# A fused attention and gated feed-forward kernel on one core: a new hand-written order for all engines, with the unread matmuls of the first block placed differently

## The chip, the cores and the metric

The kernel runs on one core of one Trainium2 chip. The metric is the device time of one execution in microseconds (us). The engines of the core are named as in the profile: PE (TensorE, the matrix engine), PEld (its weight loads, which overlap its matmuls), DVE (VectorE), ACT (ScalarE), POOL (GpSimd) and SP (SyncE, which here only issues DMAs). Each engine works through its own row of instructions in the order in which it was given them, and the engines wait for one another through semaphores.

## The reference

The computation has two stages, both in float32 at the ends. The weights arrive as float64 words. With B = H = 8, S = 576, D = 64, d_model = 512 and d_ff = 1536:

```python
k_p = k.reshape(B, H, 72, 8, D).mean(axis=3)      # keys pooled by 8: 576 -> 72
v_p = v.reshape(B, H, 72, 8, D).mean(axis=3)
scores = matmul(q, k_p.T) / sqrt(D)               # 576 x 72 per head
attn = exp(scores - max(scores)); attn /= sum(attn) + 1e-9
x = matmul(attn, v_p)                             # put together: 4608 x 512
gate = 1 / (1 + exp(-(x @ w_gate)))               # 512 -> 1536
val = x @ w_val
out = (gate * val) @ w_out                        # 1536 -> 512
```

## The kernel before, in words

**Tiling.** The 4608 tokens are cut into 9 blocks of 512. A block's attention works on four pairs p of heads (128 rows) and on two halves hf of the queries. In the code's names: `keys` (DVE sums 8 neighbours), `put` (ACT writes the pooled keys of a pair into a block-diagonal tile `kbd`), `sc` (PE's scores: 4 matmuls of 144 columns for half a block), `max` (DVE), `exp` (ACT), `sum`, `main`, `rest` (DVE: the sums of the exponentials, their reciprocals and the scaling), `turn` and `rturn` (PE's transposes), `hi`, `lo` (ACT and DVE split a float32 value in two float32r parts), `av` (PE: attention times values), `x` (ACT copies a block's x out of PSUM). A float32 product of the feed-forward stage is three float32r matmuls, high by high, high by low and low by high.

**Block 0 alone.** `first_pass` computes block 0 from attention to output, reads and converts the weights meanwhile (`lw` loads 1 MB of float64 words, `conv` and `kw` make float32r parts of it on ACT and DVE, `mm.i.f` is chunk f of the product with w_gate, i = 0, or w_val, i = 1, in four chunks; `gate.f` its sigmoid, `h.f` the product, `acc.f` the second layer), and does the attention of blocks 1 and 2. Words are written with their indices: `sc.0.1.1` is the scores of block 0, pair 1, half 1, and `first.k.i` is the first pass's load i of kind k (kind 0: the keys k0..k3; 1: the queries q0..q3; 2: a table of ones for sums over tokens; 3: block 0's values, four pieces and a rest).

**Blocks 1 to 8 in four rounds** of two blocks each. In a round the first layer is done by products of the Strassen kind: m = 1..7 for gate (G) and value (V) and for each of six pairs p of chunks, each product 6 matmuls of 512 columns into a `chain` bank. Their operands are `xo` tiles (sums of quarters of the two blocks' x, each combined on DVE, copied by ACT and split by DVE), and the weights come back from DRAM by `reload` in groups A to D into a ring of six `parts` buffers: a load waits until the product that used the buffer last is done. The second layer (`second_sums`) goes over 21 units (m, q) of 12 matmuls into `acc` banks, its weights loaded into three `oparts` buffers and its operands `hs` made by ACT and DVE, i = 0..20, two units ahead. The next round's x operands (`combine`, `parts_of`) and the attention of later blocks stand between.

**The order.** All this code doesn't issue anything by itself. Every engine instruction is recorded as a unit of a `Book`; matmuls that belong together are one unit. Buffers and PSUM banks are handed out in the order of recording, which in `first_pass` is the list of words `ORDER`. At the end the units are issued in another order, that of a table of numbers, `LATER`, one number for each unit:

```python
    with tc.manual_schedule(engines={e.engine for e in engines}):
        for n in LATER.split() or range(len(book.units)):
            for taken in book.units[int(n)]:
                taken.issue()
```

So `LATER` alone sets each engine's row, the DMA issues on SP's and POOL's included, while what a unit computes and where it puts it stay as recorded.

**The unread matmuls.** When a word of `first_pass` gets its PSUM bank, `bank_for` can record matmuls ahead of its own, 128 x 128 in float32 of a zero tile or the identity, into that same bank. Nobody reads what they write: the word's own first matmul starts the bank anew. How many is in `UNREAD`, a count by word; each is a unit of its own and leaves two records of PE in the profile.

```python
            x = kbd[RING - 1][:, :P] if now[0].startswith("sc.0") else ident
            for _ in range(UNREAD.get(now[0], 0)):
                nc.tensor.matmul((t[:, 0] if len(shape) == 3 else t)[:, :P], lhsT=x, rhs=x, start=True, stop=True)
```

Every instruction that goes through the `Book` shows in the profile with line 319, where it is issued; which one it is is told by its tiles.

## Time and profile before

| | before |
|---|---|
| runs: median of 3 (lowest to highest) | 934.22 us (932.6 to 936.99) |
| the profiled execution | 933.27 us |
| its span in the profile | 931.5 us |
| granted TensorE clock, mean | 0.999 |
| instructions | 12557 |
| PE busy | 918.0 us, 99% of the span |
| DVE busy | 695.0 us, 75% |
| ACT busy | 572.4 us, 61% |
| POOL busy | 24.1 us, 3% |

The span runs from the first to the last recorded work of the profiled execution; the 1.8 us between it and the execution's time lie around that. Busy shares are averages over the whole span, and the stages differ: what counts is read by stretches of time and from the waits of each engine. An idle time in brackets stands ahead of the instruction that ended it, with what released it.

### The profile page before, as it was taken

The numbers are of one execution on the slowest core, as the hardware profiler recorded it, in microseconds if no ns is written. First come the engines' busy times: TensorE is split into PE (matmuls) and PEld (weight loads), VectorE is DVE, ScalarE is ACT, GpSimd is POOL, SyncE is SP. The second block draws the span as 40 slices with busy tenths as digits, with TensorE's granted clock in tenths as the row PEclk, the third lists the DMA queues.
The fourth block names the chain that finished last, engine by engine and source line by source line (L and its number), as shares of the span: only waits on it lengthen the run. The fifth ranks groups of instructions, "written<-read, shape, count | busy, mean of one in ns | idle before, by whom it ended". The sixth has DMA issues, their size and how long they took to land.

```text
span 931.5 us, 12557 instructions
## 1 busy us (share of the span) xinstructions
PE 918.0 (99%) x4375; PEld 756.0 (81%) x4375; DVE 695.0 (75%) x1062; ACT 572.4 (61%) x1044; POOL 24.1 (3%) x59
## 2 busy tenths in 40 slices
PE   8999999999999999999999999999999999999998
PEld 7778788887888878888888888888888878888886
DVE  6998888899999997976789956464768573544763
ACT  7999998679989764665575636443554353234442
POOL 1000000011121000000000000000000000000000
PEclk9999999999999999999999999999999999999999
DMA  9999496778889757787667567545456675566266
GB/s 341 372 354 346 164 392 226 254 264 304 289 303 340 265 192 262 265 301 243 210 212 235 191 223 232 191 166 186 156 193 203 216 235 191 177 198 191 94 212 192
DMA packets 90367, 223.13 MB, mean 240 GB/s; under 512 B 9536, under 2 KB 28480, under 8 KB 88768
## 3 DMA queue, kind: packets, MB, share of 16 engines
q1 hardware_dynamic: 85184, 203.97, 64.9%
q0 software_dynamic: 5120, 18.35, 5.1%
q8 instruction: 35, 0.57, 0.2%
q14 instruction: 28, 0.23, 0.1%
HBM read 168.81 MB, written 53.48 MB: 239 GB/s over the span
## 4 chain that ended last, share of the span: by engine, by line
PE 92%; ACT 5%; DMA 2%; DVE 1%; issue 0%; POOL 0%; ACTq 0%; POOLq 0%
PE chain L319 54%; PE acc L319 27%; PE sc L319 4%; PE av L319 4%; PE tp L319 2%; ACT e L319 1%; DMA parts<-keptV0C 1%; DMA oparts<-keptS 1%; ACT w L319 1%; ACT L319 1%; DMA oparts<-keptO 0%; ACT raw L319 0%; ACT y L319 0%; PE vp L319 0%; ACT parts L319 0%
## 5 line engine op out<-in xcount | busy, mean ns | idle before, releaser
L319 PE MATMUL chain<-xo,parts 128*128 128x512 f32 x2316 | 558.6, 394 | 2.9 <-ACT y L319 1.4
L319 PEld LDWEIGHTS chain<-xo,parts 128*128 128x128 f32 x2316 | 427.2, 188 | 93.4 <-ACT y L319 2.1
L319 PE MATMUL acc<-hs,oparts 128*128 128x512 f32 (+1 forms) x1011 | 235.3, 390 | 0.8 <-DMA oparts<-keptO 0.5
L319 PEld LDWEIGHTS acc<-hs,oparts 128*128 128x128 f32 x1011 | 188.2, 188 | 41.6 <-issue 1.4
L319 DVE TENSOR_TENSOR hs<-h,hs 128x1024 fp32r<-128x1024 f32 x52 | 63.3, 1221 | 37.9 <-ACT hs L319 37.5
L319 ACT CAST hs<-h 128x1024 fp32r<-128x1024 f32 x52 | 54.6, 1053 | 52.6 <-PE acc L319 51.4
L319 DVE TENSOR_TENSOR y<-chain,sG 128x512 f32<-128x512 f32 x69 | 47.2, 686 | 45.6 <-PE chain L319 32.3
L319 DVE TENSOR_TENSOR y<-chain,sV 128x512 f32<-128x512 f32 x69 | 47.2, 686 | 37.3 <-PE chain L319 25.8
L319 ACT COPY sV<-chain 128x512 f32<-128x512 f32 x69 | 40.3, 586 | 52.4 <-PE chain L319 48.6
L319 ACT COPY sG<-chain 128x512 f32<-128x512 f32 x69 | 40.4, 586 | 48.3 <-PE chain L319 47.7
L319 ACT ACTIVATE gate<-y 128x512 f32<-128x512 f32 x69 | 43.2, 631 | 39.7 <-DVE y L319 35.2
L319 ACT CAST hs<-s 128x1024 fp32r<-128x1024 f32 x36 | 37.9, 1054 | 39.8 <-PE acc L319 24.2
L319 ACT ACT_TABLE_LOAD x47 | 60.3, 1283 | 1.4 <-DVE y L319 0.5
L319 DVE TENSOR_TENSOR hs<-s,hs 128x1024 fp32r<-128x1024 f32 x36 | 44.0, 1221 | 14.6 <-ACT hs L319 14.4
L319 DVE TENSOR_TENSOR h<-y,gate 128x512 f32<-128x512 f32 x69 | 47.4, 689 | 3.8 <-ACT gate L319 1.8
L319 PE MATMUL sc<-kbd,raw 128*128 128x144 f32 (+1 forms) x260 | 41.0, 295 | 1.0 <-ACT other L319 0.7
L319 PEld LDWEIGHTS sc<-kbd,raw 128*128 128x128 f32 (+1 forms) x260 | 33.5, 177 | 9.8 <-issue 2.8
L319 PE MATMUL acc<-oparts,hs 128*128 128x512 f32 x144 | 37.8, 399 | 0.1
L319 DVE TENSOR_REDUCE m<-sc 128x4 f32<-128x288 f32 x48 | 21.7, 452 | 14.3 <-PE sc L319 14.0
L319 PEld LDWEIGHTS acc<-oparts,hs 128*128 128x128 f32 x144 | 26.3, 188 | 5.5 <-ACT pr L319 0.3
L319 DVE TENSOR_TENSOR h<-h 128x256 f32<-128x256 f32 (+2 forms) x39 | 28.3, 728 | 0.7
L319 ACT ACTIVATE gate<-chain 128x512 f32<-128x512 f32 x23 | 13.8, 599 | 18.9 <-PE chain L319 18.5
(193 smaller groups left out, 1026.0 us busy)
## 6 DMA issues: line engine op xcount, KB each, us to landing
oparts<-keptS SPq DMA_DIRECT2D x48, 512.0 KB, 4.1
oparts<-keptO SPq DMA_DIRECT2D x72, 256.0 KB, 3.5
raw<-in_wgv SPq DMA_DIRECT2D x12, 1024.0 KB, 8.7
out<-o SPq DMA_DIRECT2D x35, 256.0 KB, 4.4
raw<-in_kT SPq DMA_DIRECT2D x28, 288.0 KB, 4.8
raw<-in_qT SPq DMA_DIRECT2D x29, 256.0 KB, 4.4
raw_o<-in_wo SPq DMA_DIRECT2D x12, 512.0 KB, 6.7
keptO<-oparts SPq DMA_DIRECT2D x12, 512.0 KB, 3.8
```

Source lines behind the costliest of these rows:

```text
L319: return self._book.take(lambda: f(*args, **named))
```

## The change

`ORDER`, all functions and all tiles stay as they are. Two tables are new.

`UNREAD` has other counts. In all there are 49 unread matmuls instead of 44, so the book has 3737 units instead of 3732:

```diff
 UNREAD = {
-    "sc.0.1.1": 10, "sc.0.1.0": 1, "sc.0.0.1": 1, "sc.0.2.0": 5, "sc.0.3.1": 7, "sc.0.3.0": 2, "sc.1.0.0": 1,
-    "rturn.0.1": 5, "av.0.3": 1, "mm.0.0": 1, "mm.0.1": 5, "mm.1.0": 2, "mm.1.1": 1, "mm.0.2": 1, "sc.1.1.0": 1,
+    "sc.0.1.1": 1, "sc.0.1.0": 1, "sc.0.0.1": 4, "sc.0.0.0": 2, "sc.0.2.1": 1, "sc.0.2.0": 2, "sc.0.3.1": 3,
+    "rturn.0.0": 2, "turn.0.0": 1, "turn.0.1": 4, "sc.0.3.0": 5, "av.0.0": 1, "rturn.0.1": 2, "turn.0.3": 3,
+    "turn.0.2": 2, "av.0.3": 1, "mm.0.0": 1, "av.0.2": 2, "mm.0.1": 1, "mm.1.0": 2, "mm.1.1": 2, "mm.0.2": 3,
+    "mm.1.2": 1, "sc.1.1.0": 1, "sc.1.1.1": 1,
 }
```

`LATER` is a new table throughout (its numbers can't be compared by eye, since every unit behind a changed count has another number):

```diff
 LATER = """
-2 17 15 11 34 5 10 35 19 14 6 36 12 8 3 37 18 4 7 38 16 9 39 13 28 40 41 20 42 43 24 46 58 90 25 91 92 23 26 93 94 79
...
+3705 3706 3707 3709 3713 3710 3711 3712 3714 3722 3715 3719 3720 3717 3716 3723 3721 3718 3724 3725 3728 3729 3730
+3726 3733 3735 3734 3727 3736 3731 3732
 """
```

Read back into names, the two tables put the engines' rows like this. Unread ones aside, the two rows of an engine hold the same units.

| row | before | after |
|---|---|---|
| PE, from its start | 21 unread, sc.0.1.1, sc.0.1.0, 2 unread, sc.0.0.1, sc.0.0.0, 1 unread, sc.0.2.0, sc.0.2.1, 2 unread, sc.0.3.1, sc.0.3.0 | 14 unread, sc.0.1.1, sc.0.1.0, sc.0.0.1, sc.0.0.0, sc.0.3.1, 4 unread, sc.0.2.1, sc.0.2.0, 8 unread, sc.0.3.0, turn.0.0, turn.0.1 |
| SP, from its start | k1, k0, q1, q3, q0, k2, k3, q2, lv.1.0, lw.0.0, constants, first.3.0 | k1, q1, k3, k0, q0, q2, q3, k2, first.3.4, constants, lv.1.0, first.3.0, lw.0.0 |
| DVE, from its start | keys.0.1, keys.0.0, max.0.1.1, max.0.1.0, keys.0.2 | keys.0.1, keys.0.3, keys.0.0, max.0.1.1, max.0.1.0, max.0.0.1, max.0.0.0, keys.0.2 |
| ACT, from its start (two instructions a put) | put.0.1, put.0.0, exp.0.1.1 | put.0.1, put.0.3, put.0.0, exp.0.1.1 |
| POOL, from its start | a kbd fill, then vl, vh, kbd fills | a vh fill, then the kbd fills among the others |

Of the units that were there before, unread matmuls aside, 776 of PE's 1021, 822 of ACT's 995, 871 of DVE's 1061, 371 of SP's 556 and 28 of POOL's 55 have another place in their row, on the mean 3.7, 3.2, 2.8, 1.6 and 1.8 places away. The mean is taken over a row's units that can be matched by name. Further on, these places differ: in the first pass mm.1.2 goes ahead of mm.1.3; in the second sums of the first round unit m 6, q 1 ahead of m 2, q 0; around the turn from the third to the fourth round the product G, p 0, m 5 goes into the second sums' m 7, five places ahead on PE, the load of V, p 0, group C goes twelve places ahead on SP, and two combinations with the splits of their results go between the operands i = 9 to 13 on DVE; in the last unit of the last round the bank that is copied in one piece comes last instead of the bank that is copied in halves.

## The prediction

> **What bounds the kernel now.** I read the page's engine totals first, then busy time by stage, then what the matrix engine waited for, then the first microseconds row by row.

> ```profile
> span 931.5 us, 12557 instructions
> ...
> PE 918.0 (99%) x4375; PEld 756.0 (81%) x4375; DVE 695.0 (75%) x1062; ACT 572.4 (61%) x1044; POOL 24.1 (3%) x59
> ```
> ```profile
> 10.00:60.00 50.00, 44.99 (x245) 35.52 (x245) 47.70 (x88) 47.45 (x113) 0.00 (x0) 1.00 1.02 380
> 60.00:140.00 80.00, 78.78 (x392) 64.50 (x391) 68.61 (x112) 76.73 (x157) 0.00 (x0) 1.00 0.82 300
> 140.00:310.00 170.00, 169.16 (x819) 138.68 (x818) 158.66 (x277) 142.46 (x286) 21.60 (x40) 1.00 0.80 284
> 310.00:931.50 621.50, 616.07 (x2865) 508.27 (x2863) 416.97 (x582) 302.23 (x482) 0.00 (x0) 1.00 0.63 207
> ```
> ```profile
> PE sc L319 <- ACT early L319: 1.7, 1, 1.7
> ...
> PE chain L319 <- DMA parts<-keptV0C: 0.9, 1, 0.9
> ```

> The second fence gives busy microseconds and instructions of PE, its weight loads, DVE, ACT and POOL in four stretches, then the granted clock, the DMA share and GB/s; the third PE's waits: in total, how often, the longest. PE is idle for only 931.5 - 918.0 = 13.5 us of the whole span, so a new order can win little past the early stage: from 310 us on PE lacks 5.4 us of being always busy. The stage from 10 to 140 us is another matter. ACT is busy for 47.45 of 50 and 76.73 of 80 us there, DVE for 47.70 of 50, and the DMA engines are full to 60 us; PE's busy time there still holds unread matmuls. So early on ACT sets the pace, with DVE close behind; from about 140 us PE does.

> The profiled execution took 933.27 us (span 931.5); the median of the runs is 934.22, that is 0.95 more. I sum against 933.27 and add 0.95 at the end.

> **Part 1: the head start.**

> ```profile
> 0.73 0.22 POOL L319 MEMSET kbd<- 128x144 f32 x1 [0.29 <-POOLq L1454]
> ...
> 0.89 0.20 POOL L319 MEMSET vl<- 128x128 f32 x1
> 1.01 6.94 PE L319 MATMUL sc<-kbd 128*128 128x128 f32 x42 [1.01 <-POOL kbd L319]
> 7.79 1.15 PE L319 MATMUL sc<-kbd,h 128*128 128x144 f32 x8
> 2.12 0.43 SPq L319 DMA_DIRECT2D early<-in_qT  x1
> 3.45 1.53 DVE L319 TENSOR_REDUCE early<-h 128x72 f32<-128x576 f32 x2 [2.58 <-DMA h<-in_kT]
> 8.48 0.95 DVE L319 TENSOR_REDUCE early<-sc 128x4 f32<-128x288 f32 x2 [3.50 <-PE sc L319]
> 4.30 0.53 ACT L319 ACTIVATE kbd<-early 64x72 f32<-64x72 f32 x2 [2.06 <-DVE early L319]
> 8.97 1.45 ACT L319 ACTIVATE e<-sc,early 128x72 f32<-128x72 f32 x6 [3.36 <-DVE early L319]
> ```
> ```profile
> h<-in_kT SPq DMA_DIRECT2D x4, 288.0 KB, 3.8
> h<-in_qT SPq DMA_DIRECT2D x3, 256.0 KB, 4.2
> ```
> ```profile
> 1.00:5.20 4.20, 4.19 (x19) 4.20 (x20) 1.50 (x2) 1.87 (x5) 2.02 (x14) 1.00 0.76 251
> 5.20:7.78 2.58, 2.58 (x25) 2.58 (x24) 0.00 (x0) 0.40 (x2) 0.00 (x0) 1.00 1.05 382
> ```

> The first of these fences goes engine by engine (start, length, and in brackets the idle time ahead); the second gives KB and microseconds from issue to landing. Now 21 unread matmuls (42 records) stand ahead of the first score. Its keys were placed at 4.30 + 0.53 = 4.83 us, and PE has no gap before 7.79: the fillers hold the score back, and DVE (3.50 us) and ACT (3.36 us) wait for it. The new row has 14 fillers, 28 records. PE starts 0.89 - 0.73 = 0.16 us later, since a vh fill now precedes the first kbd fill on POOL. By the two windows a record takes 4.20 / 19 = 0.22 us up to 5.2 us and (7.78 - 5.20) / (42 - 19) = 0.11 us after. So 18 records fill 1.17 to 5.2, and the other 10 take 1.1: the first scores can start at 6.3 instead of 7.8. q1 is now the second load, at about 1.2 us, and lands about 4.2 later, 5.4: in time.

> What DVE does meanwhile: keys.0.3 now precedes keys.0.0, and k0 is the fourth load (the fourth issues at 2.12; plus 3.8 to 4.2 it is there at about 6.2). keys.0.0 ends at 6.2 + 0.77 = 7.0 (half of the 1.53 us row); then the first two maxima, 0.95 us, end at 7.9. On ACT put.0.0 (0.53) runs from 7.0 to 7.5, so the first exp starts at 7.9 instead of 8.97: 1.0 us sooner, and with put.0.3, another 0.53 us of ACT's work, already behind it. That is 1.0 to 1.5 us. ACT is full from there to 140 us, so I take 1.3 us, nearer the upper end since 0.5 of it is work done in idle time. Ends: +0.5 (k2 is now the eighth load, so put.0.2 may stall the exps behind it) to -1.5.

> **Part 2: the fillers inside.** The whole table goes from 44 to 49. Less the 21 and 14 at the head, 23 stood behind the first score and 35 do now, 12 more. At 0.11 us a record and two records each they are 12 x 0.22 = 2.6 us of PE, nearly all before 60 us, where ACT is the late one and PE's 50.00 - 44.99 = 5.0 us of idle time cover them. I take 0; without that cover they cost 2.6.

> **Part 3: the rest of the first 310 us.** Of the recorded instructions 776 of PE's 1021 units (unread ones aside), 822 of ACT's 995, 871 of DVE's 1061, 371 of SP's 556 and 28 of POOL's 55 change place, by 1.6 to 3.7 places on the mean. No work is added or taken away. One cost could still change with order alone:

> ```profile
> L319 ACT ACT_TABLE_LOAD x47 | 60.3, 1283 | 1.4 <-DVE y L319 0.5
> 58.71 3.02 PE L319 MATMUL chain<-xo,parts 128*128 128x512 f32 x12 [1.12 <-ACT y L319]
> ```

> A load stands where ACT's row turns from exp to sigmoid or back. Counted along both rows the turns are equally many, so 0. The 1.12 us stall at 58.71 comes from such a turn (gate.2 stands behind the load; mm.1.3 wants its bank). The new row puts mm.1.2's four chunks (12 matmuls, as many as that 3.02 us row) between, which would cover gate.2; but the copy that mm.1.2 needs, conv.1.1's first, goes 12 places back on ACT's row, to just ahead of the same spot. I take 0, between -1.1 (covered) and +1.1 (mm.1.2 stalls instead). On SP weight load lw.0.0 (1 MB) goes three places back, behind first.3.4, the constants and first.3.0, which the first transposes and sums want; 0, since ACT reaches its first conversion only behind exps.

> **Part 4: two stalls later.**

> ```profile
> 329.39 1.88 PE L319 MATMUL acc<-hs,oparts 128*128 128x512 f32 x7 [0.53 <-DMA oparts<-keptO]
> ...
> 767.60 4.59 PE L319 MATMUL chain<-xo,parts 128*128 128x512 f32 x19 [0.87 <-DMA parts<-keptV0C]
> 760.91 0.55 SPq L319 DMA_DIRECT2D parts<-keptV0C  x1
> ```

> At 767.60 product V, p 0, m 3 waits for a load that SP issued at 760.91, once product G, p 0, m 5 had let go of the buffer. The new row does that product inside the second sums' m 7, five places ahead, and SP issues the load twelve places sooner, between the loads of m 4. It will have landed long before: -0.9. At 329.39 second sums m 2, q 0 waits for its load; now m 6, q 1 (12 matmuls) goes first, over 2 us of cover: -0.5. Late next there is m 6, q 1's own load, one place behind on SP's row; ends of the two together -1.4 and 0.

> **Part 5: the end.**

> ```profile
> 926.36 0.59 ACT L319 COPY o<-acc 128x512 f32<-128x512 f32 x1 [6.25 <-PE acc L319]
> 927.76 0.37 ACT L319 COPY o<-acc 128x256 f32<-128x256 f32 x1 [0.81 <-PE acc L319]
> 928.16 0.42 DVE L319 COPY o<-acc 128x256 f32<-128x256 f32 x1 [6.80 <-ACT o L319]
> ```

> The last two banks change places. Now the halves that ACT (0.37) and DVE (0.42, to 928.58) copy come last; in the new row the whole bank, 0.59 on ACT alone, does: about 927.76 + 0.59 = 928.35, with a store of twice the size. +0.0, ends -0.2 to +0.5.

> **Sum.** -1.3 + 0 + 0 - 0.9 - 0.5 + 0 = -2.7. Against that I allow one new stall of the size of the two in part 4, +0.7, because so many places changed: -2.0. 933.27 - 2.0 = 931.3, plus 0.95: about **932.2 us**, a gain of 0.2%. A difference under 0.5% (4.7 us) is about what measuring this kernel cannot tell from no change.

> **The rivals.**

> A. The head start is lost again. DMA runs at a share of 1.02 from 10 to 60 us, and with it late keys, values or weights end the wait instead of ACT. For it: that share, and k2 as the last key. Against it: no row of PE's list before 60 us names a DMA. Then part 1 gives 0: 932.2 + 1.3 = 933.5.

> A variant: PE loses its pace.

> ```profile
> 14.35 0.71 PE L319 MATMUL sc<-kbd 128*128 128x128 f32 x4 [1.65 <-ACT early L319]
> 14.90 1.15 PE L319 MATMUL sc<-kbd,early 128*128 128x144 f32 x8
> ```

> PE took 0.22 us a record until 4.2 us after its start, though the granted clock reads 1.00 there. With 14 fillers it could run dry around 9 to 11 us, before k2 arrives, and be slow again. In this trace 1.65 us idle did not bring it back: 8 records took 1.15 us right after. If it were, 4.2 us at half pace would lose 2.1 us: 934.3. [...]

> B. The early stage tightens by more. In 10 to 140 us PE is idle for 5.0 + 1.2 us and ACT for 2.6 + 3.3. If the new order takes away most of ACT's 5.9 us on top of part 1 and part 4, the sum is -2.7 - 4.0 = -6.7: 927.5. For it: ACT's and DVE's rows change place more than anything else there. Against it: DVE too has only 2.3 us idle from 10 to 60.

> C. Slower: DVE in the second sums.

> ```profile
> 716.00:732.00 16.00, 16.00 (x72) 13.27 (x71) 9.30 (x9) 7.08 (x9) 0.00 (x0) 1.00 0.60 190
> 719.32 1.22 DVE L319 TENSOR_TENSOR hs<-h,hs 128x1024 fp32r<-128x1024 f32 x1 [1.34 <-ACT hs L319]
> 722.04 1.22 DVE L319 TENSOR_TENSOR hs<-h,hs 128x1024 fp32r<-128x1024 f32 x1 [1.50 <-ACT hs L319]
> 761.16 1.05 ACT L319 CAST xo<-s 128x1024 fp32r<-128x1024 f32 x1 [0.61 <-DVE s L319]
> ```

> Between operands 9 and 13 of the third round the new DVE row inserts two combinations and two splits of the next blocks' x, 4 x 1.22 = 4.9 us. An operand falls due every 722.04 - 719.32 = 2.72 us and leaves 1.50 idle; four gaps hold 6.0 us, so it fits with 0.28 us to spare each. It fails if a split waits for its ACT copy (1.05) with operands queued behind it: two chains of 1.22 + 1.05 + 1.22 are 7.0 us, all on PE, which is busy for 16.00 of 16.00 us there. 932.2 + 7.0 = 939.2. It decides once operands come later than they are used, about one period of 2.7 us. Against it: the copies stand ahead of those operands' on ACT's row too.

> **How the numbers follow.** My forecast (about -2, 930 to 933.3) 0.42; A with its variant 0.24; B 0.2; C, or a stall of that size elsewhere by the same queueing, 0.14. B lies under 929.5 in most of its span, C over 938.9 in most of its own: faster by over 0.5% 0.2, slower 0.11, between 0.69. The range from 927.8 to 937.8 leaves out about half of B and of C.

> **What would show it.** Right: the first score's row near 6.3 us, the first exp near 8, the 0.87 and 0.53 stalls gone, table loads x47, the same busy time per engine. Wrong: PE waiting on DMA or on put.0.2 before 15 us for longer than now; hs rows of DVE that end later than PE wants them around 720 us; or rows of 144 columns at 0.22 us apart, which would be the pace.

## The result and the profile after

The changed kernel takes **928.19 us** (median; 926.56 to 928.97), the kernel before 934.45 beside it: a ratio of 0.9929, 95% interval 0.9915 to 0.9942, faster by 0.7%. 932.2 was forecast. The profiled execution took 928.46 us, 4.8 less than the one of before (933.27).

The page's engine totals, and busy time by stage (columns as in the prediction: length, then PE, weight loads, DVE, ACT, POOL, then clock, DMA share, GB/s), after the change:

```profile
span 926.7 us, 12572 instructions
...
PE 916.0 (99%) x4385; PEld 758.3 (82%) x4385; DVE 695.3 (75%) x1062; ACT 572.2 (62%) x1044; POOL 24.0 (3%) x59
```
```profile
10.00:60.00 50.00, 47.68 (x272) 39.50 (x273) 47.60 (x86) 47.48 (x107) 0.00 (x0) 1.00 1.02 386
60.00:140.00 80.00, 79.74 (x401) 66.09 (x399) 70.47 (x114) 78.21 (x161) 0.00 (x0) 1.00 0.84 305
140.00:310.00 170.00, 169.31 (x824) 140.22 (x823) 160.17 (x283) 144.52 (x293) 21.57 (x40) 1.00 0.82 288
310.00:926.70 616.70, 610.96 (x2846) 504.69 (x2844) 413.11 (x574) 297.08 (x470) 0.00 (x0) 1.00 0.64 207
```

PE is busy for 916.0 instead of 918.0 us although it has ten more records of unread matmuls. So 2 of the 4.8 us are gone from busy time, which a sum over idle time cannot see. Behind 57.6 us, where neither order has an unread matmul left and the work is the same, PE needs 4.7 us less, and only 2.0 of them were idle time. The reason stands in two rows after, a group of the page (count, busy us, mean ns of one) and a row of the timeline:

```profile
L321 PE MATMUL chain<-xo,parts 128*128 128x512 f32 x2316 | 558.8, 394 | 1.8 <-DMA parts<-keptG3A 1.0
```
```profile
415.93 11.17 PE L321 MATMUL chain<-xo,parts 128*128 128x512 f32 x48
```

A 512-column matmul's record lasts 394 ns, but 48 of them in a row take 11.17 us, 0.233 each. The record reaches some 0.16 us beyond the start of the next one, and a wait of up to that length shows as busy.

PE's waits after, and its first microseconds:

```profile
PE tp L321 <- DMA cst<-in_const: 1.0, 1, 1.0
PE chain L321 <- DMA parts<-keptG3A: 1.0, 1, 1.0
PE tp L321 <- DVE early L321: 0.7, 1, 0.7
PE acc L321 <- DMA oparts<-keptS: 0.6, 1, 0.6
```
```profile
1.15 5.44 PE L321 MATMUL sc<-kbd 128*128 128x128 f32 x28 [1.15 <-POOL kbd L321]
6.43 1.15 PE L321 MATMUL sc<-kbd,h 128*128 128x144 f32 x8
8.04 1.25 PE L321 MATMUL sc<-kbd,h 128*128 128x144 f32 x8 [0.46 <-ACT kbd L321]
...
10.94 1.13 PE L321 MATMUL tp<-cst 128*128 128x128 f32 x8 [1.00 <-DMA cst<-in_const]
11.91 1.15 PE L321 MATMUL sc<-kbd,h 128*128 128x144 f32 x8
...
14.10 1.38 PE L321 MATMUL sc<-kbd 128*128 128x128 f32 x10 [0.38 <-ACT early L321]
```

The waits of 1.12 (gate 2), 0.87 (V, p 0, C), 0.53 and 0.7 us (attention of block 2) are gone. The first score starts at 6.43 us, the 28 records before it end just there, and unread matmuls now lie where PE stood idle for 1.65 us.

**Where the time went.** The same products can be found in both traces. At some places all of PE's work ahead, unread matmuls aside, is the same set in both orders. The table gives the time between the ends of such work, worked out from the matmul records of every kernel profiled below that has the old or the whole new order in the stretch and no joint of two orders in it (e6 and e9, which lack unread matmuls, are left out up to 69.6 us); times in the first column are those of the kernel before. From 178.3 to 694 us e3 and e5, whose joint lies right at the start, count as old, and e8, which moves two products there, as new. Left out as near a joint are e1 from 26.7 to 57.6 us, e5 from 69.6 to 178, e2 from 114 to 178 and e4 and e7 from 863 us on; counting them moves no mean by over 0.1 us.

| stretch of PE (us) | old order: mean (lowest to highest, n) | new order | difference |
|---|---|---|---|
| to the end of the first score, 8.4 | 8.85 (8.44 to 9.19, 4) | 7.22 (6.54 to 7.96, 6) | -1.63 |
| 8.4 to 26.7 | 18.27 (18.27 to 18.27, 4) | 19.18 (18.59 to 20.32, 6) | +0.91 |
| 26.7 to 57.6 | 30.90 (30.86 to 30.95, 4) | 31.17 (31.15 to 31.18, 6) | +0.26 |
| 57.6 to 69.6 | 12.02 (12.00 to 12.04, 4) | 10.70 (10.69 to 10.71, 6) | -1.31 |
| 69.6 to 114.0 | 44.40 (44.39 to 44.41, 4) | 43.12 (43.10 to 43.15, 7) | -1.28 |
| 114.0 to 178.3 | 64.32 (64.28 to 64.34, 4) | 63.06 (63.03 to 63.09, 7) | -1.26 |
| 178.3 to 694 | 516.3 (514.9 to 518.1, 7) | 514.7 (514.1 to 515.4, 6) | -1.65 |
| 694 to 863 | 169.8 (169.5 to 170.3, 6) | 168.5 (168.2 to 169.0, 5) | -1.33 |
| 863 to the last matmul | 64.9 (64.4 to 65.7, 6) | 64.8 (64.5 to 65.0, 4) | -0.1 |

In sum -7.4 us, against -6.3 and -7.5 in the medians of two comparisons. The head as a whole (to 57.6 us) gives 0.5; three stretches between 58 and 178 us give 3.85 and repeat to 0.1 us; the rest, 3.1, lies where weights are reloaded, and varies from execution to execution.

### The profile page after: what moved, and what is told of

It reads as the page before. It is cut to its first block, busy times and chain, and to the rows that moved or that the text cites. A ratio compares the mean times of both kernels' runs of the same rounds, so it can differ in the third digit from the quotient of the medians.

```text
span 926.7 us, 12572 instructions
## 1 busy us (share of the span) xinstructions
PE 916.0 (99%) x4385; PEld 758.3 (82%) x4385; DVE 695.3 (75%) x1062; ACT 572.2 (62%) x1044; POOL 24.0 (3%) x59
## 4 chain that ended last, share of the span: by engine, by line
PE 90%; ACT 3%; DMA 3%; DVE 2%; issue 1%; SPq 0%; ACTq 0%; DVEq 0%
PE chain L321 53%; PE acc L321 27%; PE av L321 4%; PE sc L321 3%; PE tp L321 2%; DMA parts<-keptG3A 1%; DMA oparts<-keptS 1%; DMA cst<-in_const 1%; DMA parts<-keptG1A 1%; DMA oparts<-keptO 1%; SPq L321 0%; ACT L321 0%; ACT parts L321 0%; ACT early L321 0%; ACT w L321 0%
## 5 line engine op out<-in xcount | busy, mean ns | idle before, releaser
L321 PE MATMUL acc<-hs,oparts 128*128 128x512 f32 x1011 | 235.1, 390 | 0.7 <-DMA oparts<-keptS 0.6
L321 ACT ACT_TABLE_LOAD x47 | 60.3, 1283 | 2.7 <-PE chain L321 1.3
L321 DVE TENSOR_TENSOR h<-chain,gate 128x512 f32<-128x512 f32 x23 | 15.8, 688 | 24.1 <-PE chain L321 18.0
## 6 DMA issues: line engine op xcount, KB each, us to landing
oparts<-keptO SPq DMA_DIRECT2D x72, 256.0 KB, 3.4
out<-o SPq DMA_DIRECT2D x35, 256.0 KB, 3.9
raw<-in_kT SPq DMA_DIRECT2D x28, 288.0 KB, 4.5
raw<-in_qT SPq DMA_DIRECT2D x29, 256.0 KB, 4.2
```

The lines of the kernel that those rows point to most:

```text
L321: return self._book.take(lambda: f(*args, **named))
```

## The experiments

Every unit is the same in both orders, so that a kernel can follow one table for a part of the units and the other for the rest. Where two orders meet, a wait of its own can arise.

**e1: the new head alone.**

```diff
-LATER: the old table
+LATER: the first 63 units of the new table, then the old order of the rest
-UNREAD: 21 ahead of the first score, 44 in all
+UNREAD: 14 ahead of the first score, 34 in all
```

> Every engine follows the new table up to the new row's fourth score (about the first 9 us: 14 unread matmuls ahead, the new order of the first loads, keys and puts) and the old one from there; 34 unread matmuls in all. Theory: the scores start 1.2 to 1.4 us sooner, ACT keeps about 0.8 us of it: the time falls by 0.8 us. Rival 1 (the prediction's part 1 as it stands): by 1.3 us. Rival 2 (the head start is lost again to the loads or to the pace): by 0.

Measured: 936.95 us (before 934.64), ratio 1.0025 (1.0014 to 1.0037): slower. None of the three had this sign. PE's rows, and the stages with the granted clock:

```profile
6.98 2.44 PE L310 MATMUL sc<-kbd,h 128*128 128x144 f32 x16
11.83 1.25 PE L310 MATMUL sc<-kbd,h 128*128 128x144 f32 x8 [2.42 <-ACT kbd L310]
14.62 1.22 PE L310 MATMUL sc<-kbd 128*128 128x128 f32 x4 [1.54 <-ACT early L310]
15.63 2.13 PE L310 MATMUL sc<-kbd,early 128*128 128x144 f32 x8
```
```profile
11.00:13.00 2.00, 1.17 (x8) 1.03 (x8) 1.12 (x3) 1.99 (x11) 0.00 (x0) 1.00 1.01 427
13.00:15.00 2.00, 0.46 (x3) 0.39 (x3) 1.88 (x3) 1.82 (x9) 0.00 (x0) 0.61 0.98 381
15.00:17.00 2.00, 2.00 (x10) 2.00 (x10) 1.93 (x6) 2.00 (x4) 0.00 (x0) 0.50 1.07 418
17.00:19.00 2.00, 2.00 (x9) 1.71 (x8) 1.36 (x3) 0.26 (x1) 0.00 (x0) 0.50 1.08 408
```

PE got through its early work, stood idle for 2.42 and 1.54 us with 1.25 us of work between, and the granted clock fell to 0.50 until 20.28 us: eight score records took 2.13 us instead of 1.15. The stretch from 8.4 to 26.7 us took 21.64 instead of 18.27 us. This is the variant of rival A of the prediction (PE loses its pace), brought on by the head without the unread matmuls that the changed kernel has behind it. The clock fell at 13.46 us, 0.38 us into the second gap, and no single gap there was longer than 2.42 us.

**e2, e3: the new order up to 70 and up to 178 us, the old one behind.**

```diff
-LATER: the old table; UNREAD: the old counts
+LATER: the first 490 (e2) or 1154 (e3) units of the new table, then the old order; UNREAD: the new counts
```

> New table up to about 70 us (the 119th of PE's units, unread ones aside), old table from there. Theory: what PE had gained at 70 us in the changed kernel, 1.35 us, is kept, since PE is all but never idle behind it: the time falls by 1.2 to 1.6 us, and the wait of 1.12 us for gate 2 near 58 us is gone. Rival: the two orders do not fit together and the gain needs the rest of the new order too: by 0 or slower.

> New table up to about 178 us (the first pass but for its last products), old table from there. Theory: the gain of 3.9 us that PE has at that place in the changed kernel stays to the end, with the old stalls of 0.53 and 0.87 us back: the time falls by 3.6 to 4.2 us, which is most of the whole gain and is the prediction's rival B. Rival: the later order is needed to use it (operands and weights come late for a PE that is early): by 1 to 2.5 us only.

Measured: e2 935.41 us, ratio 1.0008 (0.9994 to 1.0021); e3 931.12 us, 0.9958 (0.9945 to 0.9971). In e2 PE is 1.24 us ahead at 70 us, and a wait of 1.1 us for ACT at the joint takes it back at once: as a time, e2 decides nothing. e3's median falls by 3.5 us, a little under the theory's 3.6 and under the 4.3 to which the table's stretches up to 178 us add up. The first 178 us are worth about half of the whole gain or a little more; they are not all of it.

**e4, e7: the late part.** e4 has the new order only from 694 us, e7 all of it but that part.

```diff
-LATER: the old table (e4), the new table (e7)
+LATER: e4: the first 3169 units of the old table, then the new order; e7: the first 3172 of the new table, then the old order
```

> Old table up to about 694 us (the end of the third round's products), new table from there: the turn from the third to the fourth round and the end. Theory: the stall of 0.87 us and 0.2 us around it go (-1.1), the last unit of the end costs 0.36: the time falls by 0.7 us. Rival (the prediction's rival C: combinations and splits ahead of the operands hold PE up): slower by 2 us or more.

> The changed kernel up to about 694 us, the old order from there. Against 928.2 us. Theory: the stall of 0.87 to 1.27 us for the load of V, p 0, C comes back, the end is 0.4 us better: +0.5 to +1.0, 928.7 to 929.2. Rival (as the kernel with only the late part new came out 1.65 us slower than before): the new late part costs, and without it the time falls to 926.5 to 927.5.

Measured: e4 936.29 us, ratio 1.0018 (1.0010 to 1.0027), slower; e7 930.85 us, 0.9951 (0.9933 to 0.9969), beside 0.9929 for the whole change. So taking the late part away costs some 2 us, and adding it alone costs 1.65. Both have waits at the joint that neither whole order has (in e7 0.68 us for the copy sV and 0.9 us for DVE's y), so neither time is the late part's own. What is free of joints is the stretch from 694 to 863 us in the table: -1.33. In every profile with the old order there PE waits for V, p 0, C, 0.21 to 1.27 us; in none with the new order. e4's first 694 us are the same as before's, yet its profile is 2.9 us later there: waits of 0.85 us at 258 (an attention product that waits for DVE), 0.44 at 396 and 0.37 at 489 us (two loads), which the first profile of before did not have. That was not expected, and e10 takes it up.

**e5: the new order from 57 to 178 us alone.**

```diff
-LATER: the old table
+LATER: the old table to the last matmul of mm.0.0 (57.6 us), the new order to 178 us, the old order behind
```

> Old tables to about 57 us (44 unread matmuls, the old head), the new order from there to about 178 us, the old order after. Against 934.6 us before. Theory: the whole gain that lasts is made between 57 and 178 us, where the new order takes away waits of 1.12, 0.71 and 0.25 us of PE and as much again hidden in rows counted as busy; head and unread matmuls give nothing: about -3.7 us, 931, as much as the kernel that follows the new table from the start to 178 us (931.1). Rival (the prediction's part 1): the head is worth 1.3 us of it: -2.4, 932.2.

Measured: 933.87 us (before 935.28), 0.9982 (0.9970 to 0.9995). Only -1.4. The trace shows why: the joint costs 2.15 us (57.6 to 69.6 us takes 14.17 instead of 12.02; PE waits 1.91 us there, and the clock is at 0.50 for 3.41 us behind it), but the next two stretches take 43.11 and 63.07, as in the changed kernel. So those two gains, 1.29 and 1.25 us, need neither the new head nor the new unread matmuls. For the stretch from 57.6 us this can't be said.

**e6: without the 12 unread matmuls between the scores 0.3.1 and 0.3.0.**

```diff
-    "rturn.0.0": 2, "turn.0.0": 1, "turn.0.1": 4, "sc.0.3.0": 5,
+    (none of these)
```

> The changed kernel without the 12 unread matmuls between the scores 0.3.1 and 0.3.0 (37 instead of 49). Against 928.2 us. Theory: PE then stands idle for about 2.0 and 2.3 us of the stretch from 9.9 to 15.3 us, the granted clock falls to 0.5 as in the kernel with the new head alone, and PE is 2 to 3 us late at 21 us; some 1.5 to 3 us remain at the end: 929.7 to 931. Rival 1 (they are only ballast): the clock stays at 1.00 and the time is the same or up to 2.6 us less. Rival 2: the clock falls, but ACT, which sets the pace, hides it: 928.2.

Measured: 929.44 us, 0.9933 (0.9912 to 0.9954). The profiled execution kept its clock, with these gaps:

```profile
8.36 1.25 PE L310 MATMUL sc<-kbd,h 128*128 128x144 f32 x8 [1.25 <-ACT kbd L310]
...
11.54 1.25 PE L310 MATMUL sc<-kbd,h 128*128 128x144 f32 x8 [1.44 <-ACT kbd L310]
13.84 0.76 PE L310 MATMUL sc<-kbd,early 128*128 128x144 f32 x4 [1.05 <-ACT early L310]
15.56 0.66 PE L310 MATMUL tp<-cst,pm 128*128 128x128 f32 x4 [0.97 <-DVE pm L310]
```

The six executions fall in two groups: mean clock 1.00 and 926.77 and 927.63 us, or 0.994 to 0.996 and 928.19 to 931.19 us (mean 930.2). So with the clock kept the twelve are worth next to nothing (rival 1), and they keep the clock from falling, which costs about 3 us (the theory); only one of the two groups has a profile, so the gaps of the other are not known. In the changed kernel all six executions read 0.999 or 1.0.

**e9: without the 23 unread matmuls behind the score 0.3.0.**

```diff
-    "av.0.0": 1, "rturn.0.1": 2, "turn.0.3": 3, ... "sc.1.1.1": 1   (14 words, 23 matmuls)
+    (none of these)
```

> The changed kernel without the 23 unread matmuls that stand behind the score 0.3.0 (22 to 45 us), 26 instead of 49. They take about 23 x 0.22 = 5 us of PE. Theory (part 2 of the prediction): PE waits for ACT there anyway, so they are covered: PE is less than 0.3 us earlier at 57 us and the time is the same as the changed kernel's, 928.0 to 928.6, with the clock at 1.00. Rival 1 (ballast on PE, which shows 25.00 of 25 us busy from 35 to 60): 1.5 to 3 us faster. Rival 2: the gaps take the clock, 2 us or more slower.

Measured: 928.34 us, 0.9922 (0.9909 to 0.9936), the same as the changed kernel's 0.9929 and 0.9921. The profiled execution, at 928.60 us, shows a piece of rival 2 (the two rows of PE and one stage of e9, then the same stage of the changed kernel behind its longer one from 35 to 60 us):

```profile
37.07 0.51 PE L309 MATMUL chain<-xo,parts 128*128 128x512 f32 x1 [1.33 <-ACT xo L309]
38.39 5.87 PE L309 MATMUL chain<-xo,parts 128*128 128x512 f32 x18 [0.81 <-DVE xo L309]
```
```profile
38.00:42.00 4.00, 3.61 (x9) 2.86 (x10) 3.93 (x6) 2.93 (x6) 0.00 (x0) 0.57 0.94 297
```
```profile
35.00:60.00 25.00, 25.00 (x127) 20.36 (x126) 24.37 (x41) 24.53 (x42) 0.00 (x0) 1.00 1.01 385
...
38.00:42.00 4.00, 4.00 (x19) 3.28 (x18) 4.00 (x6) 3.81 (x7) 0.00 (x0) 1.00 0.93 305
```

Without the 5 us of unread work PE waited instead, the clock stood at 0.50 for 3.41 us (0.57 is the mean of the four), and the stretch from 26.7 to 57.6 us took 32.29 instead of 31.17 us. Where the clock is kept (927.09 to 928.89 us in the runs at 1.00) nothing is gained either: PE's 25.00 of 25 us from 35 to 60 us in the changed kernel are no sign that PE set the pace there. That leaves ACT (24.53) and DVE (24.37).

**e8: two edits for a faster version.**

```diff
-PE: G p3 m5, G p3 m1, av, av (second round); the end of the new table
+PE: av, av, G p3 m5, G p3 m1; from 907 us the old order
```

> The changed kernel with two edits: the two attention products of block 5 (1.0 us of PE) go ahead of product G, p 3, m 5 of the second round, which waited 0.97 us for its load, and from about 907 us the old order with its old end. Against 928.2 us. Theory: the wait shrinks to under 0.2 us and the end gives 0.3: 927.0 to 927.4. Rival: load waits differ from one execution to the next, so that taking one away in the trace does not show in the median: 928.0 to 928.4.

Measured: 928.79 us, 0.9930 (0.9913 to 0.9947): no faster than the changed kernel. The wait for G3A is not in e8's profile (one of 0.68 us, for a copy by ACT, stands two products later instead), but neither is it in those of e6, e7, e9 and e11, which have that order unedited. The rival was right: it was one execution's.

**e10, e11: both kernels once more**, each with another profile, without an edit.

> The kernel before, once more with a profile of its own. Theory: its median is 934.5 to 935.3; the profile shows other load waits of PE behind 178 us than the first one (2.5 us in all there, in a run 1.4 us under the median), 3 to 4.5 us in all, and a first score that moves by up to 1 us. Rival: waits and first score repeat to 0.2 us.

> The changed kernel, once more with a profile of its own. Theory: median 928.0 to 929.0; up to 178 us the same steps against the kernel before (-1.28 at 58 to 69, -1.28 at 86 to 114, -1.05 at 124 to 178 us), behind it load waits of 1.8 to 2.5 us. Rival: the later order too saves nothing in the mean, load waits of 3 us or more.

Measured: before 935.18 us (0.9999, 0.9989 to 1.0010, against itself); changed 927.35 us, 0.9921 (0.9905 to 0.9938). From e10's list of PE's waits, and PE's first rows of e10 and of e11:

```profile
PE chain L310 <- DVE y L310: 1.2, 1, 1.2
PE acc L310 <- DMA oparts<-keptO: 1.1, 2, 0.8
...
PE chain L310 <- DMA parts<-keptV0C: 0.9, 1, 0.9
...
PE acc L310 <- DMA oparts<-keptS: 0.8, 2, 0.4
```
```profile
1.01 7.62 PE L310 MATMUL sc<-kbd 128*128 128x128 f32 x42 [1.01 <-POOL kbd L310]
8.46 1.15 PE L310 MATMUL sc<-kbd,h 128*128 128x144 f32 x8
```
```profile
1.15 4.89 PE L310 MATMUL sc<-kbd 128*128 128x128 f32 x28 [1.15 <-POOL kbd L310]
5.88 1.15 PE L310 MATMUL sc<-kbd,h 128*128 128x144 f32 x8
8.53 1.25 PE L310 MATMUL sc<-kbd,h 128*128 128x144 f32 x8 [1.50 <-ACT kbd L310]
```

Behind 178 us PE's gaps over 0.1 us, most of them for loads, add up to 4.45 us here and to 2.48 in the first profile of the same kernel, which was 1.2 us under its median: the theory. The same 42 records took 7.62 instead of 6.94 us, the same 28 records 4.89 instead of 5.44. In the changed kernel the gaps behind 178 us add up to 2.50 and 1.79 us.

## Why the prediction was right or wrong

The time lies in the forecast range, but only 0.4 us above its lower end, and the second comparison's 927.35 lies below that end. The likeliest case gave a third of the gain: -2.0 forecast, -6.3 and -7.5 measured. That the range held is owed to its width and not to the sum. In size it is rival B (927.5), which had 0.2; its reason holds only in part. And the change is no borderline case, as the prediction had it for anything under 0.5%: the interval of the ratio is 0.27% wide.

- **Part 1, the head (-1.3 forecast, about -0.5 measured).** The scores came sooner as forecast (6.43 us against 6.3; first score -1.63 in the mean), and the first exp at 8.18 against 7.9. The time itself is partly a draw, since it hangs on when the first matmuls come to full pace (last section): where that happens at 5.20 us (before) and 5.28 us (e7), the old head's first score starts at 7.79 and the new one's at 6.34, which is the forecast 1.5. That the head start would last was the step that failed: 0.9 us are lost again by 27 us and 0.3 by 58. The scores behind the first two now wait for k0's keys (0.46 us after, 1.50 in e11, not at all in e2 and e7), which is rival A's late load in small. The sign named for that, PE waiting for a DMA before 15 us, came too: the 1.00 us at 10.94. But it is four unread matmuls that wait there for the constants, and the score behind them starts at 11.91 us, against 11.54 in e6, which lacks them.
- **Part 2, the fillers inside (0 forecast).** Right as time: e9 and e6 gain nothing without them while the clock holds. But their use was missed: I counted a price and no effect. They hold the clock (without twelve of them four of e6's six executions read 0.994 to 0.996), and the head of e1, which lacks most of those ahead of the score 0.3.0, costs 2.3 us. The variant of rival A named the mechanism and put it at 2.1 us for the wrong kernel.
- **Part 3 (0 forecast, -3.85 measured).** This is the mis-sized term. I gave the 1.12 us wait at 58.71 us bounds of -1.1 and +1.1 and took the middle. The new order covers it:

```profile
53.71 6.54 PE L321 MATMUL chain<-xo,parts 128*128 128x512 f32 x28
```

In it mm.1.2 runs ahead of mm.1.3 without a gap, since ACT now does gates 0 and 2 there ahead of the next conversions. In 70 to 114 us block 2's scores 2.2.1 and 2.2.0 stood back to back and waited 0.13 and 0.71 us; in the new order 5 us of other work lie between them. From 114 to 178 us only 0.25 of 1.26 us was visible as idle. The rows before:

```profile
105.26 0.76 PE L319 MATMUL sc<-kbd,raw 128*128 128x144 f32 x4 [0.71 <-ACT other L319]
...
130.11 3.00 PE L319 MATMUL chain<-xo,parts 128*128 128x512 f32 x12 [0.25 <-ACT y L319]
```

What the records hide shows from start to start. Taking as usual the lower quartile of the spacing between records of the same two shapes in the same trace, PE was behind the usual by 2.40, 3.21 and 3.10 us in the three stretches before and by 1.12, 2.14 and 1.97 after, which is most of the 3.85. Delays of 1.40 us at mm.1.3, 0.88 at score 2.2.0, 0.60 at mm.1.9 and 0.31 at mm.1.8 are gone after. I took PE's 1.2 us of idle time between 60 and 140 us for about all that PE could gain there, and the busy column hid nearly as much again as it showed. No single move was run alone: the stretches and the waits that went are shown, and which move took which wait away is only argued from the rows.
- **Rival B's reason** (ACT's idle time shrinks): ACT's idle time from 10 to 140 us went from 2.6 + 3.3 to 2.5 + 1.8 us, so 1.6 us of the 4.0 that I had priced. PE's own waits were the larger part.
- **Part 4 (-1.4 forecast, about -3.0 measured).** The two named waits went: no profile with the new order shows either. In the mean of the profiles with the old order they are 0.87 us (V, p 0, C) and 0.34 (m 2, q 0; two of seven lack it), so 1.2 of the 3.0 us; which waits make up the rest was not traced. The load of V, p 0, C is issued long before it is needed:

```profile
742.50 0.33 SPq L321 DMA_DIRECT2D parts<-keptV0C  x1
```

That is 18 us sooner than before's 760.91, where PE itself runs only some 5 us ahead. What was missed is that the first profile shows only one draw of the load waits: over seven profiles with the old order the stretch from 178 to 694 us spreads over 3.2 us, with the new order over 1.4, 1.65 lower in the mean. The allowance of +0.7 for a new stall is about what G1A's wait near 582 us costs (0.3 to 0.8 us in five of the six profiles with the new order there).
- **Rival C** did not come about. DVE's row has only short gaps there, 0.83 us the longest, and PE does not wait on it; 0.38 us for a split at 756 us in e6 is all that any profile without a joint there shows:

```profile
719.59 1.23 DVE L321 TENSOR_TENSOR hs<-h,hs 128x1024 fp32r<-128x1024 f32 x1 [0.83 <-ACT hs L321]
720.73 1.22 DVE L321 TENSOR_TENSOR xo<-s,xo 128x1024 fp32r<-128x1024 f32 x1
```

- **Part 5 (0 forecast)** and the 47 table loads came as forecast: behind the last matmul both orders take 3.76 to 3.79 us (4.83 in e1).

Still open: which moves make the stretch from 114 to 178 us shorter, and why e4, whose first 694 us are before's, was later there in its profile and 1.65 us slower in the median; the draws of the load waits alone may not explain the second.

## What to carry to other kernels

Judge a new instruction order by stretches between places where the same work is done, in several profiles of each kernel, not by idle time: the matmul records here overlap (0.394 us long, 0.233 apart), and a short wait is partly booked as busy. Price each wait of the bounding engine that the new order touches, also when the sum of idle time looks small, and look at what the new order puts in front of it. Unread work on the matrix engine should be counted as what holds the clock, as it did here (1.00 in two of six executions without twelve of the matmuls, 0.999 or 1.0 in all six with them): the question is which gaps are left if it goes, not what it costs.

## What the runs showed of the hardware

How long the first matmuls run at half pace differs between executions of the same kernel too. The clock's record begins, with 1.00, between 4.01 us (e9) and 7.31 us (e8) in the thirteen profiles (5.20 before, 5.48 after), and in each the first records go from 0.22 to 0.11 us apart within 0.1 us of that; ahead of it nothing is recorded, and the views print 1.00. So the first score of the old head ended between 8.44 and 9.19 us, that of the new one between 6.54 and 7.96. That is a spread of 3.3 us in the change of pace and of up to 1.4 us in the first score; no run shows what sets the moment.
